# Linear attention and an MLP in one kernel: v of the first wave loaded and cast by the GpSimd queue

## The chip, the core and the metric

The kernel runs on one core of a Trainium2 chip. A core has a matrix engine (PE, with its weight loads shown apart as PEld), a vector engine (DVE), an activation engine (ACT), a general engine (GpSimd, POOL in the profile) and a sync engine (SP) that only issues transfers. The metric is the device time of one launch in microseconds, lower is better. Each engine works through its own list of instructions in order; an instruction may wait for another engine or for a transfer.

## What is computed

A causal linear attention with decay over 4 batches, 8 heads, 768 positions and 64 channels, and on its output an MLP of 512 to 2048 to 512:

```python
for b in range(nb):                      # blocks of 64 positions
    intra = np.einsum('bhic,bhjc->bhij', qb, kb) * Dmask[None]
    intra = np.einsum('bhij,bhjd->bhid', intra, vb)
    inter = np.einsum('bhid,bhde->bhie', qb * lam_pow[None], kv_state)
    out[:, :, sl] = intra + inter
    kv_state = lam_block * kv_state + np.einsum('bhsd,bhse->bhde', kb * rev_pow, vb)
x = out.transpose(0, 2, 1, 3).reshape(B * S, H * D)
h = x @ w_in
return (h * (1.0 / (1.0 + np.exp(-1.702 * h)))) @ w_out
```

Inputs and output are float32; the kernel multiplies in bf16.

## The kernel before

The positions are cut into six waves of 128 (NW = 6), and the 3072 rows of the MLP come 512 to a wave. Waves 0 and 1 are special (ND = 2): each holds the first 256 positions of two batches, called c = 0 and c = 1 in the code ("batch 0" and "batch 1" of the wave below). In them partition s holds the positions 2s and 2s + 1 next to each other, so that a transfer reads runs of 128 floats; a stands for the parity of the position. Waves 2 to 5 hold 128 positions of all four batches.

A pair (w, c) of the first two waves goes through these steps. `load_one` (L76) brings k, q and v as float32 on the SP queue; in wave 0 each comes in two halves of four heads (L79, L81), but v of batch 1 whole. `do_cast` (L193, L200) multiplies k and q by powers of the decay and writes bf16 (`ks`, `qs`). `cast_v` (L218) writes v in bf16 to `v_sb`, whose layout is partition, block, head, channel, with 2c + a as block: two copies, one for each parity, on the engines it is given (ACT at L216, GpSimd at L210). `turn_pe` (L227, L233) transposes `ks` and `qs` on PE and copies the result to `kT`, `qT`. `d_scores` (L246, L254) multiplies k by q and masks the product on DVE (`sm`, L258). `d_state` (L262, L269) makes the state from `ks` and v, for the first half of the positions and for all; `d_keep` (L275) copies it to `kv_sb` on ACT. `d_out` (L277) multiplies the masked scores by v (L284) and the state by q (L289), and `d_x` copies the sum to `xT`. Then the MLP can start for that batch's columns: `mlp1_half` (L370, L378) makes two of the 16 groups of hidden columns for half of the wave's rows, `mlp1` (L360, L366) one group for all, and `mlp2` (L384, L390) the output.

The order of work is written out by hand. Under `manual_schedule` the head (L432 to L485) lists wave 0 instruction by instruction; after it a list of side tasks with due places among the MLP's items sets the order (L506 to L537). `fill(n)` (L136, L140) issues n matmuls on zeros that nothing reads; they stand in the head where PE would else be idle.

Transfers are issued from two queues in the main: SP takes k, q, v, the DMA transposes of later waves and the stores; GpSimd takes the MLP's weights, which are cast from float32 to bf16 by the transfer (`load_w_in` L176, five pieces; `load_w_out` L181, four). Two gates hold a queue back: `gate_pool(x)` (L424) lets GpSimd read one element of x, so that what stands behind it on GpSimd starts when x is there; `gate_sync(x)` (L427) does it on SP with a tiny transfer. In the head GpSimd makes the masks and identity (L109 to L132), waits at the gate for the first half of v of batch 0 (L444), issues the first piece of w_in, casts k of batch 1 (L452), issues two pieces of w_in, casts one parity of v of batch 1, and then issues all other weights. SP loads all of wave 0 at once (L104) and waits before wave 1 until the second piece of w_out is there (L477).

Of the kernel before, what the change touches and what calls it, by code (L numbers as in the profile page):

```python
# [24 lines left out]
def kernel(  # L25
# [13 lines left out]
    nc = tc.nc  # L39
    f32 = mybir.dt.float32  # L40
    bf16 = mybir.dt.bfloat16
    B, H, S, D = q.shape
    P = 128
# [19 lines left out]
    const = ctx.enter_context(tc.tile_pool(name="const", bufs=1))  # L63
# [25 lines left out]
    def load(w, nms="kqv"):  # L89
        src = {"k": k, "q": q, "v": v}  # L90
        if w < ND:
            for c in range(HF):
                for nm in nms:
                    load_one(w, c, nm, src[nm])
        else:
            for nm in nms:
                for c in range(HF):
                    load_one(w, c, nm, src[nm])
# [2 lines left out]
    nc.scalar.dma_start(out=lam_r, in_=bass.AP(tensor=lam.tensor, offset=lam.offset, ap=[[0, 1], [1, H]]))  # L101
    ones = const.tile([1, P], f32)
    nc.vector.memset(ones, 1.0)
    load(0)  # L104

    nc.scalar.preload_act_table_set("natural_log_exp_and_others")

    def iota(x, pattern, base, cm):
        nc.gpsimd.iota(x, pattern=pattern, base=base, channel_multiplier=cm, allow_small_or_imprecise_dtypes=True)  # L109

    A, Z = slice(0, 64), slice(64, P)
    zero = const.tile([P, W], bf16)
# [3 lines left out]
    i_qd = const.tile([P, 2], f32)  # L116
    iota(i_qd[A], [[1, 2]], 1 - 2 * P, 2)
    iota(i_qd[Z], [[1, 2]], 1 - P, 2)
    ident = const.tile([P, P], bf16)
    make_identity(nc, ident)  # L120
    mask_d = const.tile([P, 1, 2, 2, D], bf16)
# [41 lines left out]
    mk_pow(blk_pow, 1.0 * P)  # L163
    warm = const.tile([P, 1], f32)

    v_sb = [const.tile([P, B, H, D], bf16, name=f"v_sb{i}") for i in range(2)]
    kv_sb = [const.tile([P, B, NP, P], bf16, name=f"kv{i}") for i in range(2)]

    CW = 4
# [45 lines left out]
    def act_copy(out, in_):  # L215
        nc.scalar.copy(out, in_)  # L216

    def cast_v(w, c, copies=(pool_copy, pool_copy)):  # L218
        f = loaded.pop((w, c, "v"))
        dst = v_sb[w % 2]  # L220
        if w < ND:
            for a in range(2):
                copies[a](dst[:, 2 * c + a], f.rearrange("p h (a d) -> p h a d", a=2)[:, :, a, :])
        else:
            copies[0](dst[:, 2 * c : 2 * c + 2].rearrange("p b h d -> p (b h d)"), f.rearrange("p h e -> p (h e)"))
# [34 lines left out]
            masked[w, c, pp, h] = sm  # L260

    def d_state(w, c, full, tag="a"):  # L262
        ks, vt, b = cast[w, c, "k"], v_sb[w % 2], 2 * w + c
        t, rows = acc("ps_kv", shape=[P, NP, D], tag=tag), slice(0, P) if full else A
        for r in range(NP):
            for a in range(2):
                for h, hs in enumerate((A, Z)):
                    n0 = r * P + h * D
                    nc.tensor.matmul(t[hs, r, :], ks[rows, a, n0 : n0 + D], vt[rows, 2 * c + a, 2 * r + h, :],  # L269
                                     start=(a == 0), stop=(a == 1))  # L270
        return t, b, 0 if full else 1

# [2 lines left out]
            nc.scalar.copy(kv_sb[i][hs, b, :, hs], t[hs, :, :])  # L275

    def d_out(w, c, tag="a"):  # L277
        vt, b = v_sb[w % 2], 2 * w + c
        oa, oz = acc("ps_o", tag=tag), acc("ps_o", tag=tag)
        for r in range(NP):  # L280
            for a in range(2):
                for t, bs in ((oa, A), (oz, Z)):
                    for h, hs in enumerate((A, Z)):
                        nc.tensor.matmul(t[hs, r, :], vt[bs, 2 * c + a, 2 * r + h, :],  # L284
                                         masked[w, c, r // 2, h][bs, r % 2, a, :], start=(r + a == 0),
                                         stop=(t is oa and a == 1), skip_group_check=True)
        for r in range(NP):
            for hs in (A, Z):
                nc.tensor.matmul(oz[hs, r, :], kv_sb[1][:, b, r, hs], q_of(w, c, slice(0, P), r, 1), start=False, stop=True,  # L289
                                 skip_group_check=True)  # L290
        if w not in xT:
            xT[w] = xp.tile([P, NP, W], bf16, tag="x", name="xT")
        return oa, oz
# [130 lines left out]
    def gate_pool(x):  # L424
        nc.gpsimd.tensor_copy(behind_q, x)
# [4 lines left out]
    with tc.manual_schedule():  # L430
        u32 = mybir.dt.uint32
        for x in kv_sb:  # L432
            nc.vector.memset(x.rearrange("p b r s -> p (b r s)").bitcast(u32), 0)
        nc.scalar.activation(warm, q_pow[:, 0, 0:1], GELU)
        fill(5)
        for g in range(2):
            do_cast(0, 0, "k", nc.vector, g)
            turn_pe(0, 0, "k", act_copy, g)
            fill(2)
        for g in range(2):  # L440
            do_cast(0, 0, "q", nc.vector, g)
            turn_pe(0, 0, "q", act_copy, g)
            fill(2 - 2 * g)
        gate_pool(loaded[0, 0, "v"][0:1, 0, 0:1])  # L444
        load_w_in(0)
        cast_v(0, 0, (act_copy, act_copy))
        d_scores(0, 0, 0)
        fill(1)
        d_scores(0, 0, 1)
        fill(3)  # L450
        for g in range(2):
            do_cast(0, 1, "k", nc.gpsimd, g)  # L452
        for j in (1, 2):
            load_w_in(j)
        one = d_state(0, 0, False, "mm")
        two = d_state(0, 0, True, "mm")
        fill(1)
        d_keep(*one)
        d_keep(*two)
        oa, oz = d_out(0, 0, "mm")  # L460
        d_x(0, 0, 0, oa, act_copy)
        d_x(0, 0, 1, oz, act_copy)
        do_cast(0, 1, "q", nc.vector, 0)
        do_cast(0, 1, "q", nc.vector, 1)
        turn_pe(0, 1, "k", dve_copy)
        turn_pe(0, 1, "q", act_copy, 0)
        fill(2, True)
        turn_pe(0, 1, "q", act_copy, 1)
        fill(2)
        cast_v(0, 1, (act_copy, pool_copy))  # L470
        for j in range(3, len(IN_CH)):
            load_w_in(j)
        for j in range(NCH):
            load_w_out(j)
        nc.gpsimd.affine_select(mask, mask, pattern=[[0, 1], [1, P]], channel_multiplier=-1, base=0,
                                compare_op=mybir.AluOpType.is_ge, fill=0.0)
        gate_sync(w_out_sb[1][0:1, 0, 0:2])  # L477
        load(1)
        d_scores(0, 1, 0)
        mlp1_half(0, 0, 0)  # L480
        d_scores(0, 1, 1)
        fill(1)
        one = d_state(0, 1, False)
        two = d_state(0, 1, True)
        d_keep(*one)  # L485

        def finish(w, c, two=None):
            oa, oz = d_out(w, c)
            d_x(w, c, 0, oa, act_copy)
            d_x(w, c, 1, oz, dve_copy)  # L490
            if two:
                d_keep(*two)

        def start(w, c):
            for pp in range(2):
                d_scores(w, c, pp)
            d_keep(*d_state(w, c, False))

        def end(w, c):
            finish(w, c, d_state(w, c, True))  # L500

        def stores():
            for f in late:
                f()

        side, main = [(0, (finish, 0, 1, two))], []  # L506
        for w in range(NW):
            n = len(main)
            main += mlp_items(w)
            e = len(main)  # L510
            x = w + 1
            if x < ND:
                for c in range(HF):
                    t, d = n + 24 + 5 * c, n + 19 + 7.5 * c
                    side += [(d, (do_cast, x, c, "k", nc.vector)), (d + 1 + 0.5 * c, (do_cast, x, c, "q", nc.vector)),
                             (d, (cast_v, x, c)),
                             (t, (turn_pe, x, c, "k", (act_copy, dve_copy)[c])),
                             (t + 1 + c, (turn_pe, x, c, "q", (act_copy, dve_copy)[c])),
                             (t + 3, (start, x, c)), (t + 6 - c, (end, x, c))]
            elif x < NW:  # L520
                for c in range(HF):
                    tk, tq = (n + 2.1 + 2 * c, n + 4 + c) if x == ND else (n + 4 + 2 * c, n + 5 + 2 * c)
                    side += [(tk, (do_cast, x, c, "k", nc.vector)), (tk, (turn_dma, x, c, "k")),
                             (tq, (do_cast, x, c, "q", nc.vector)), (tq, (turn_dma, x, c, "q")),
                             (n + 6 + 2 * c, (cast_v, x, c))]
                if x == ND:
                    side += [(n + 7, (stores,))]
                t = n + 16
                side += [(t, (n_two, x, 0)), (t + 4, (n_two, x, 1)), (t + 9, (n_rest, x))]
            if w + 2 < NW:  # L530
                side += [(n + (12 if w else 20), (load, w + 2))]
        side.sort(key=lambda x: x[0])
        for i, (f, *a) in enumerate(main):
            while side and side[0][0] <= i:
                _, (g, *b) = side.pop(0)
                g(*b)
            f(*a)  # L537
# [30 lines left out]
```

## Time and profile before

| what | us |
|---|---|
| median of 5 runs | 210.99 |
| the five runs | 210.83 to 212.99 |
| the profiled execution | 211.34 |
| its span, first to last instruction | 209.3 |
| ACT casts of v (L216), three | 0.62 each |
| GpSimd cast of v (L210), 128 x 512 | 0.61 |
| load of k or q of 256 KB on SP, issue to landing, median | 3.3, 5.5 |
| w_in pieces on GpSimd, issue to landing in the head | 5.0 to 9.5 |

The profile is one execution, 0.35 us above the median. A line of its timeline has the start and the duration in microseconds, the engine, the line of the kernel, the operation, what is written and read, how many instructions are merged, and in brackets how long the engine was idle before and what released it. The "chain that ended last" is followed back from the last instruction; it names PE for 90% of the span, the two full MLP lines alone for 70%. In the head it runs through the fillers, the transposes, the qT copy, the scores, the state and its copy, the output and the first MLP matmuls, and PE waits in the head for nothing longer than 0.5 us once it has begun.

### The profile page before, as it was taken

What the parts mean: (1) busy time and instruction counts of PE and PEld (TensorE: products, weight loads), DVE (VectorE), ACT (ScalarE), POOL (GpSimd) and SP (SyncE); (2) the same over time, 40 slices, a digit from 0 to 9 for tenths busy, and PEclk for the clock granted to TensorE, in tenths of its full rate; (3) what the DMA queues carried; (4) which work ended last, traced back from release to release, by engine and by line L of the source; (5) the groups of instructions that cost most, each with busy time, mean ns of one, the idle gap of its engine ahead of it and who ended that gap; (6) DMA issues with size and microseconds to landing.
All of it is one profiled execution on the core that took longest, in us unless ns stands there. A gap on an engine that the chain in (4) does not pass through costs nothing.

```text
span 209.3 us, 4272 instructions
## 1 busy us (share of the span) xinstructions
PE 201.7 (96%) x1810; PEld 107.7 (51%) x1835; DVE 94.6 (45%) x134; ACT 85.3 (41%) x156; POOL 24.2 (12%) x41
## 2 busy tenths in 40 slices
PE   7989999999999999999999999999999999999994
PEld 2567544557864464444464444464444464444453
DVE  5575000589931838851748720748720741100121
ACT  5886662223765030466030466030466021466000
POOL 4287000111030000510003000021000000000000
PEclk9999999999999999999999999999999999999999
DMA  5999999999998899999998499990480021100112
GB/s 144 303 246 199 202 207 262 290 263 213 189 203 169 186 231 215 229 187 172 223 217 196 138 180 214 228 247 2 135 168 0 24 81 50 50 0 3 50 50 100
DMA packets 87640, 33.82 MB, mean 162 GB/s; under 512 B 67398, under 2 KB 84678, under 8 KB 87622
## 3 DMA queue, kind: packets, MB, share of 16 engines
q1 hardware_dynamic: 82868, 29.37, 66.9%
q0 software_dynamic: 4752, 4.19, 12.6%
q8 instruction: 14, 0.23, 0.5%
q14 instruction: 4, 0.03, 0.0%
q10 hardware_dynamic: 2, 0.00, 0.0%
HBM read 27.26 MB, written 6.29 MB: 160 GB/s over the span
## 4 chain that ended last, share of the span: by engine, by line
PE 90%; DVE 5%; DMA 1%; issue 1%; ACT 1%; DVEq 0%
PE ps_out L390 37%; PE ps_h L366 33%; PE ps_h L378 5%; PE ps_fill L140 4%; PE ps_s L305 2%; PE ps_o L351 2%; PE ps_o L354 2%; PE ps_t L233 2%; DMA qT<-qs 1%; DVE o_sb L394 1%; DVE sm L258 1%; PE ps_o L284 1%; PE ps_s L254 1%; PE ps_kv L269 1%; PE ps_kv L329 1%
## 5 line engine op out<-in xcount | busy, mean ns | idle before, releaser
L390 PE MATMUL ps_out<-w_out,g_sb 128*128 128x512 bf16 (+2 forms) x400 | 83.8, 362 | 1.2 <-issue 0.8
L366 PE MATMUL ps_h<-xT,w_in 128*128 128x512 bf16 x330 | 73.2, 379 | 0.3
L368 ACT ACTIVATE g_sb<-ps_h 128x512 bf16<-128x512 f32 x84 | 50.2, 597 | 47.8 <-PE ps_h L366 47.8
L390 PEld LDWEIGHTS <-g_sb 128*128 128x128 bf16 x416 | 38.2, 98 | 41.0
L366 PEld LDWEIGHTS <-w_in 128*128 128x128 bf16 x336 | 32.9, 98 | 39.2
L394 DVE COPY o_sb<-ps_out 128x512 f32<-128x512 f32 (+2 forms) x26 | 16.9, 650 | 45.6 <-PE ps_out L390 45.5
L312 DVE SCALAR_TENSOR_TENSOR sm<-ps_s,inv_pow,mask 128x512 bf16<-128x512 f32 x32 | 21.8, 743 | 32.7 <-PE ps_s L305 24.7
L210 POOL CAST v_sb<-vf 128x1024 bf16<-128x1024 f32 (+1 forms) x13 | 12.4, 966 | 111.0 <-DMA vf<-in_v_dram 110.0
L358 ACT CAST xT<-ps_o 128x512 bf16<-128x512 f32 x16 | 8.2, 599 | 36.8 <-PE ps_o L354 36.8
L334 DVE SCALAR_TENSOR_TENSOR kv<-kv,blk_pow,ps_kv 64x256 bf16<-64x256 bf16 x24 | 11.5, 480 | 7.8 <-PE ps_kv L329 4.7
L200 DVE TENSOR_TENSOR ks<-kf,kd_pow 128x512 bf16<-128x512 f32 (+1 forms) x4 | 3.7, 955 | 18.9 <-DMA kf<-in_k_dram 17.6
L258 DVE TENSOR_TENSOR sm<-ps_s,mask_d 128x512 bf16<-128x512 f32 x16 | 10.0, 684 | 3.4 <-PE ps_s L254 3.2
L378 PE MATMUL ps_h<-xT,w_in 128*128 128x256 bf16 x96 | 11.3, 273 | 0.0
L205 DVE TENSOR_TENSOR ks<-kf,k_pow 128x1024 bf16<-128x1024 f32 x8 | 10.6, 1325 | 0.1
L205 DVE TENSOR_TENSOR qs<-qf,q_pow 128x1024 bf16<-128x1024 f32 x8 | 10.6, 1322 | 0.0
L140 PE MATMUL ps_fill<-zero 128*128 128x512 bf16 x22 | 8.8, 511 | 1.4 <-DVE zero L113 1.4
L378 PEld LDWEIGHTS <-w_in 128*128 128x128 bf16 x96 | 8.9, 98 | 1.7 <-DMA w_in<-in_moe_w_in_dram 0.2
L380 ACT ACTIVATE g_sb<-ps_h 128x512 bf16<-128x512 f32 x12 | 7.2, 597 | 4.7 <-PE ps_h L378 4.5
L351 PE MATMUL ps_o<-qT,kv 128*64 128x128 bf16 x128 | 7.7, 220 | 0.4
L351 PEld LDWEIGHTS <-kv 128*64 128x64 bf16 x128 | 7.0, 110 | 1.7 <-issue 1.7
L354 PE MATMUL ps_o<-sm,v_sb 128*64 128x128 bf16 x128 | 7.6, 219 | 0.0
L275 ACT CAST kv<-ps_kv 64x256 bf16<-64x256 f32 x16 | 5.9, 367 | 3.2 <-PE ps_kv L269 3.0
(59 smaller groups left out, 91.6 us busy)
## 6 DMA issues: line engine op xcount, KB each, us to landing
vf<-in_v_dram SPq DMA_DIRECT2D x11, 512.0 KB, 7.5
kf<-in_k_dram SPq DMA_DIRECT2D x10, 512.0 KB, 6.2
qf<-in_q_dram SPq DMA_DIRECT2D x10, 512.0 KB, 7.4
out_dram<-o_sb SPq DMA_DIRECT2D x15, 256.0 KB, 2.0
out_dram<-o_sb SPq DMA_DIRECT2D x17, 128.0 KB, 2.5
w_out<-in_moe_w_out_dram POOLq DMA_DIRECT2D x4, 512.0 KB, 14.0
w_in<-in_moe_w_in_dram POOLq DMA_DIRECT2D x3, 512.0 KB, 8.0
kf<-in_k_dram SPq DMA_DIRECT2D x4, 256.0 KB, 3.3
```

What stands on the lines that cost most here:

```text
L140: nc.tensor.matmul(fill_ps[0], zero[:, 0:P], zero, start=True, stop=True)
L205: eng.tensor_tensor(x.rearrange("p b (h d) -> p b h d", h=H), f.rearrange("p (b h) (a d) -> p b (h a) d", b=2, a=2), pw.unsqueeze(3).to_br ...
L210: nc.gpsimd.tensor_copy(out, in_)
L258: nc.vector.tensor_tensor(sm.rearrange("p i a s -> p i (a s)"), s2[h].rearrange("p (i a) s -> p i (a s)", i=2), mask_d.rearrange("p o a b ...
L312: nc.vector.scalar_tensor_tensor(sm, s, inv_pow[:, 2 * p + h : 2 * p + h + 1], mask.to_broadcast([P, B, P]), op0=MUL, op1=MUL)
L351: nc.tensor.matmul(ps_o[hs, b, :], kv[:, b, p, hs], qT[:, (b % 2) * NP + p, :], start=(b == 0), stop=False, skip_group_check=True)
L354: nc.tensor.matmul(ps_o[hs, b, :], vt[:, b, 2 * p + h, :], masked[w, p, h][:, b, :], start=False, stop=True, skip_group_check=True)
L366: nc.tensor.matmul(h, w_in_sb[j][:, kc, i * P : (i + 1) * P], xT[w][:, kc, :], start=(kc == 0), stop=(kc == KC - 1))
L368: nc.scalar.activation(g_of[w][:, fc, :], h, GELU)
L378: nc.tensor.matmul(h[:, u, :], w_in_sb[j][:, kc, i * P : (i + 1) * P], xT[w][:, kc, cols], start=(kc == 0), stop=(kc == KC - 1))
L390: nc.tensor.matmul(ps_out, g_of[w][:, fc, g * P : (g + 1) * P], w_out_sb[j][:, fc % CW, c0:c1], start=(fc == 0), stop=(fc == FFC - 1))
L394: nc.vector.tensor_copy(o, ps_out)
```

## The change

Three things change, all in wave 0. v of both batches is no longer loaded by SP and cast by ACT and GpSimd: a transfer on the GpSimd queue (`load_v`) casts it and writes it to `v_sb[0]`. It is written as it lies in memory, so that in wave 0 the parity stands inside the head, and `d_v` picks the matching slice for the matmuls. The first such transfer stands after GpSimd's iotas for q, the second behind a gate on the second half of k of batch 0; the gate before the first piece of w_in is on the second half of q of batch 0, where it was on v. SP loads k and q of batch 0, then k and q of batch 1, each in two halves. The list for batch 1 of wave 0 is also written in another order: both halves of q are transposed one after the other, two fillers come off there, the second scores stand ahead of the first `mlp1_half`, and the filler behind them comes off.

```diff
-    load(0)
+    load(0, "kq")
...
+    v_sb = [const.tile([P, B, H, D], bf16, name=f"v_sb{i}") for i in range(2)]
+
+    def load_v(c):
+        nc.gpsimd.dma_start(out=v_sb[0][:, 2 * c : 2 * c + 2].rearrange("p a h d -> p (a h d)").rearrange(
+            "p (h e) -> p h e", h=H), in_=v[c, :, 0 : 2 * P, :].rearrange("h (s a) d -> s h (a d)", a=2))
...
     iota(i_qd[Z], [[1, 2]], 1 - P, 2)
+    load_v(0)
...
+    def d_v(w, c, a, hd):
+        x = v_sb[w % 2][:, 2 * c : 2 * c + 2].rearrange("p a h d -> p (a h d)")
+        return x.rearrange("p (h a d) -> p a h d", h=H, a=2)[:, a, hd] if w == 0 else v_sb[w % 2][:, 2 * c + a, hd]
...
-                    nc.tensor.matmul(t[hs, r, :], ks[rows, a, n0 : n0 + D], vt[rows, 2 * c + a, 2 * r + h, :],
+                    nc.tensor.matmul(t[hs, r, :], ks[rows, a, n0 : n0 + D], d_v(w, c, a, 2 * r + h)[rows],
...
-                        nc.tensor.matmul(t[hs, r, :], vt[bs, 2 * c + a, 2 * r + h, :],
+                        nc.tensor.matmul(t[hs, r, :], d_v(w, c, a, 2 * r + h)[bs],
...
-        gate_pool(loaded[0, 0, "v"][0:1, 0, 0:1])
+        gate_pool(loaded[0, 0, "k"][0:1, H - 1, 0:1])
+        load_v(1)
+        gate_pool(loaded[0, 0, "q"][0:1, H - 1, 0:1])
         load_w_in(0)
-        cast_v(0, 0, (act_copy, act_copy))
...
         turn_pe(0, 1, "q", act_copy, 0)
+        turn_pe(0, 1, "q", act_copy, 1)
         fill(2, True)
-        turn_pe(0, 1, "q", act_copy, 1)
-        fill(2)
-        cast_v(0, 1, (act_copy, pool_copy))
...
         d_scores(0, 1, 0)
+        d_scores(0, 1, 1)
         mlp1_half(0, 0, 0)
-        d_scores(0, 1, 1)
-        fill(1)
```

## The prediction

> **What bounds the kernel now.** I read the page's busy shares first, then its 40 slices, then the timeline of the TensorE (PE) and of GpSimd (POOL) from 8 to 20 us, and last the DMA queues in narrow windows. Page, parts 1 and 2 (a digit is tenths of a 5.2 us slice):
>
> ```profile
> PE 201.7 (96%) x1810; PEld 107.7 (51%) x1835; DVE 94.6 (45%) x134; ACT 85.3 (41%) x156; POOL 24.2 (12%) x41
> PE   7989999999999999999999999999999999999994
> DMA  5999999999998899999998499990480021100112
> ```
>
> PE is busy 96% of 209.3 us, and all digits below 9 except the last lie in the first three slices. From about 19 us on, MLP matmuls run back to back to the end, so whatever moves the start of that run moves the end by as much. The change touches only what lies before it, and there the DMA row is at 9 as well. PE's timeline there (start, duration, engine, line, operation, count, and in brackets the idle time before):
>
> ```profile
> 10.22 0.82 PE L140 MATMUL ps_fill<-zero 128*128 128x512 bf16 x3
> 10.97 0.81 PE L269 MATMUL ps_kv<-v_sb,ks 64*64 64x64 bf16 x32
> 12.25 0.64 PE L284 MATMUL ps_o<-sm,v_sb 64*64 64x128 bf16 x32 [0.47 <-ACT kv L275]
> 14.50 0.59 PE L140 MATMUL ps_fill<-zero 128*128 128x512 bf16 x2
> 15.03 0.42 PE L254 MATMUL ps_s<-qT,kT 64*64 64x128 bf16 x16
> 15.47 1.05 PE L378 MATMUL ps_h<-xT,w_in 128*128 128x256 bf16 x8
> 16.80 0.39 PE L140 MATMUL ps_fill<-zero 128*128 128x512 bf16 x1
> 18.95 1.27 PE L378 MATMUL ps_h<-xT,w_in 128*128 128x256 bf16 x10
> ```
>
> See that no long hole is left: fillers (L140) stand directly before ps_kv, the first user of v. The run that must not stop begins at 18.95 (19.01 in the chain of waits). Now the loads. GpSimd's timeline, and ACT's v casts:
>
> ```profile
> 8.23 0.18 POOL L425 COPY behind_q<-vf 1x1 f32<-1x1 f32 x1 [4.85 <-DMA vf<-in_v_dram]
> 8.35 0.92 POOL L178 DMA_DIRECT2D w_in<-in_moe_w_in_dram  x1
> 10.13 2.04 POOL L200 TENSOR_TENSOR ks<-kf,kd_pow 128x512 bf16<-128x512 f32 x2 [0.86 <-DMA kf<-in_k_dram]
> 12.12 1.55 POOL L178 DMA_DIRECT2D w_in<-in_moe_w_in_dram  x2
> ...
> 9.70 1.14 ACT L216 CAST v_sb<-vf 128x512 bf16<-128x512 f32 x2
> ```
>
> And the queues' packets (count, MB, share), first 9.3 to 12 us, then 13 to 14, then 14 to 16:
>
> ```profile
> q1 hardware_dynamic: 1553, 0.77, 120.3%
> q0 software_dynamic: 3, 0.00, 0.4%
> ...
> q0 software_dynamic: 247, 0.13, 92.2%
> q1 hardware_dynamic: 217, 0.10, 45.5%
> ...
> q0 software_dynamic: 733, 0.38, 141.2%
> ```
>
> q1 is SP's queue, q0 GpSimd's. The first w_in had been issued at 9.27, yet to 12 us only 3 packets of it moved against 1553 of SP's; GpSimd's queue came in as SP's ran dry.
>
> **The change, part by part.**
>
> (1) SP's list falls from twelve units of 256 KB to eight (v's four go). 1553 packets in 2.7 us are 575 per us, so a unit of 512 packets takes 0.89 us. Today the eighth unit is batch 1's k, second half, in place when GpSimd's second cast of it began at 11.1. So SP's queue would end near 11.0 instead of 14.2 if nothing else shared the engines. Bytes read stay the same: the 1 MB of v now goes through GpSimd's queue.
>
> (2) Two v loads on GpSimd's queue, 1024 packets each of 512 B read and 256 B written; no row shows that form. Nearest rows: w_in's 1 KB reads, 733 packets in 2 us on 16 engines, 44 ns per packet and engine; 2 KB reads (20 to 30 us, 2041 packets), 78 ns; SP's own 512 B, 28 ns. These lie on one line in bytes read, so I take 28 ns: 64 packets per engine, 1.8 us a load. Lower end 19 ns (the write alone, half the bytes on that line), upper 59 (double and more, if the cast has a fixed price). Issue cost on GpSimd: 0.75 us for 512 packets, so 0.75 to 1.5 each; I take 1.2. The first is put after the iotas (1.31), and pushes identity, mask_d, i_k, i_q, mask to about 4.6: identity is first needed at 5.84, i_k by ACT at 5.02, mask_d at 9.73. Covered; without this cover up to 1.2 us. The second stands behind a gate on k's second half (landed by 5.4) and ahead of the w_in gate, now on q's second half (cast at 7.29) where it was on v's first (8.23). So w_in is issued about 0.8 earlier, but queues behind both v loads; GpSimd's k casts and later weight loads follow as before.
>
> (3) ACT loses three v casts (1.14 + 0.62), GpSimd one (0.61). Before ps_kv the ACT casts end at 10.84, the fillers at 11.04: the gain on the path is nothing, the fillers cover it. The later casts (14.42 to 15.81) end before 17.12, where their user starts: nothing again, except that GpSimd issues later weights 0.6 us earlier. Weights have slack: the fourth column group of w_in is needed at 21.6.
>
> (4) Three fillers less (two before L254 at 15.03, one at 16.80), 0.216 us each: 0.65 off the path. What is late next: the second scores need ACT's qT copy, done at 15.29, some 0.15 later than PE would be there. Net -0.5 if every load is where it is today. The second scores also stand ahead of the first half MLP now; its w_in (15.47 today) is then needed only at about 15.7.
>
> (5) v inside the head by parity: PE's reads stay 64 elements contiguous and the counts are equal. Zero.
>
> When does the first v land? Here **rule and row differ**. The row: w_in issued at 8.35, moving from 12, 3.7 us later, only as SP's queue emptied. The Trainium skill ("DMA: Bandwidth & Descriptors", Queues, rings and completion order; and Latency and other measured facts) says that each DMA engine goes round-robin between queues packet by packet, and gives about 1 us to the first byte for the GpSimd path; it also says that issuing from several engines adds no bandwidth. By the rule v alternates with k and q and delays both; by the row it waits for them. Taking the row: v flows freely from about 11.0, less some 0.4 us of it moved where SP leaves room (4.5 to 5.5 us: 424 packets against 623 per us just after), plus 1.8 and 0.3 for completion: 12.7, and 12.3 if the tails overlap as at 13 to 14 us. I take 12.3. Then ps_kv starts 1.3 after its 11.04. Batch 1's k and q have landed long before, so the rest follows at PE's pace: +1.3 - 0.65 + 0.25 (ACT's kv, xT and qT copies now run right behind one another) = **+0.9**. Second v 14.2, first w_in 15.7, needed at 17: no further wait.
>
> The profiled execution is 209.3 of span in 211.34; the five runs have the median 210.99, 0.35 lower. I add to the median: 211.9.
>
> The **clock** is the second place. The PE rows show the first fillers at 0.43 us and those from 8 us on at 0.21; the granted clock says 1.00 throughout. The skill ("TensorE: Matmul & The Clock Gate", The HAM clock gate) has the array fall back to half rate after an idle window of about 3.4 us. PE's new hole, 11.0 to 12.3, is far under that, so I charge nothing; by an idle window it would be up to 1.7 us more.
>
> **Rivals.**
>
> *B: the queues alternate.* v reaches the engines at 1.31 + 3.75 = 5.1. From there about 165 of SP's packets per engine are left, and alternate with 64 + 64 of v and 32 of w_in: 128 x 56 ns + 32 x 72 ns = 9.5, so batch 1's q, second half, lands at about 15.2 instead of 12.1. Then cast 0.65, transposes 0.3, fillers and copy 0.7, scores 0.4, half MLP 1.05, states 0.74, outputs 1.08: 20.3, **+1.3**, 212.3. For it: the rule, and 29 packets against 532 from 12 to 13. Against: 3 against 1553.
>
> *C: v slips in where SP leaves room.* If v comes by 10.9 and q stays under 13.5, only the fillers count: **-0.5**, 210.5. For it: DMA at half in the first slice, and the dip at 4.5.
>
> *S: slower, the price of a cast packet.* With 59 ns a v load is 3.8 us: v at 14.5, 18.3, first w_in 19.7, then 1.05 + 0.74 + 1.08: 22.6, **+3.6**, 214.6. It passes 1% from about 54 ns. Against: the three rows on one line.
>
> *It doesn't do what it says* is A itself: v "straight to its place" later than by way of ACT.
>
> **How the numbers follow.** A 0.42 (211.9), B 0.23 (212.3), C 0.20 (210.5), S 0.13 (214.6), 0.02 for something faster that I don't see. One per cent, 2.1 us, is about what a measurement of this kernel can tell from no change. Slower than 213.1: most of S (0.11) and 0.05 from A or B with a slow clock, 0.16. Faster than 208.9: 0.02. Within: 0.82. The range takes C less 0.3 at the bottom and B plus 1.0 (a price of 44 ns, or part of a cold window) at the top: 210.2 to 213.3.
>
> **What would show it.** Right if ps_kv's first matmul waits for v's DMA until about 12.3, SP's last head load is issued by about 6.5, and the first full MLP group starts near 19.9. B: DVE waits for q of batch 1 past 14. C: no wait before ps_kv. S: w_in lands after 17. Wrong altogether if the span grows after 25 us, in a stage that I hold untouched.

## The result, and the profile after

The changed kernel takes 212.65 us in the median of 44 runs (211.84 to 213.98), the kernel before on the same chips 211.58 (79 runs, 210.65 to 215.73). The ratio is 1.0049, with a 95% interval from 1.0035 to 1.0064: about 1.04 us are lost, less than one per cent. Ratios, here and below, leave out runs more than 1.5% above the fastest of their kernel. The forecast of +0.9 us was right in size (its 211.9 stood on a base of 210.99 from five runs, and the base is 211.58), and its mechanism was not: this is rival B. The profiled execution of the changed kernel took 212.98 us, with a span of 211.2 (before: 211.34 and 209.3). That pair differs by 1.64 because the one lies 0.33 above its median and the other 0.24 below its own.

The page of the changed kernel, parts 1 and 2:

```profile
PE 200.3 (95%) x1807; PEld 106.9 (51%) x1832; DVE 93.8 (44%) x134; ACT 83.5 (40%) x153; POOL 25.6 (12%) x43
PE   7588999999999999999999999999999999999993
DMA  5999999999999899999996399990480011100112
```

PE has 1.4 us less to do and the span is 1.9 us longer. In PE's row the second digit falls from 9 to 5 and the fourth from 9 to 8, and from the fifth on only the last differs: the loss lies in the first four slices, 21 us. The timeline of the changed kernel there, PE first, then DVE, then GpSimd:

```profile
8.89 0.40 PE L243 MATMUL ps_t<-ident,qs 128*128 128x128 bf16 x4 [1.39 <-DVE qs L206]
10.72 0.40 PE L243 MATMUL ps_t<-ident,qs 128*128 128x128 bf16 x4 [0.99 <-DVE qs L206]
12.14 0.82 PE L147 MATMUL ps_fill<-zero 128*128 128x512 bf16 x3
12.89 0.81 PE L279 MATMUL ps_kv<-v_sb,ks 64*64 64x64 bf16 x32
16.30 0.40 PE L243 MATMUL ps_t<-ident,qs 128*128 128x128 bf16 x4 [0.37 <-DVE qs L206]
17.72 1.05 PE L388 MATMUL ps_h<-xT,w_in 128*128 128x256 bf16 x8
20.75 2.79 PE L388 MATMUL ps_h<-xT,w_in 128*128 128x256 bf16 x24
...
8.14 0.69 DVE L206 TENSOR_TENSOR qs<-qf,qd_pow 128x512 bf16<-128x512 f32 x1 [2.08 <-DMA qf<-in_q_dram]
9.97 0.69 DVE L206 TENSOR_TENSOR qs<-qf,qd_pow 128x512 bf16<-128x512 f32 x1 [1.13 <-DMA qf<-in_q_dram]
15.55 0.69 DVE L206 TENSOR_TENSOR qs<-qf,qd_pow 128x512 bf16<-128x512 f32 x1 [0.41 <-DMA qf<-in_q_dram]
...
1.47 1.06 POOL L114 DMA_DIRECT2D v_sb<-in_v_dram  x1 [0.15 <-issue]
4.79 0.92 POOL L114 DMA_DIRECT2D v_sb<-in_v_dram  x1
10.08 0.62 POOL L435 COPY behind_q<-qf 1x1 f32<-1x1 f32 x1 [4.36 <-DMA qf<-in_q_dram]
10.65 0.75 POOL L184 DMA_DIRECT2D w_in<-in_moe_w_in_dram  x1
```

And the casts of q in the kernel before, from its DVE timeline:

```profile
6.35 0.69 DVE L200 TENSOR_TENSOR qs<-qf,qd_pow 128x512 bf16<-128x512 f32 x1 [0.29 <-DMA qf<-in_q_dram]
7.29 0.69 DVE L200 TENSOR_TENSOR qs<-qf,qd_pow 128x512 bf16<-128x512 f32 x1 [0.25 <-DMA qf<-in_q_dram]
12.13 1.28 DVE L200 TENSOR_TENSOR qs<-qf,qd_pow 128x512 bf16<-128x512 f32 x2
```

`ps_kv`, the first user of v, stands directly behind its fillers with no bracket: it waits for no v. What is late is q. DVE waits for all the halves of q shown; the two of batch 0 are cast at 8.14 and 9.97 (before 6.35 and 7.29), and the last one of batch 1 at 15.55 (before, both halves of batch 1 were cast in one stretch that ended at 13.41). The gate for w_in, which the change put on q, opens at 10.08. GpSimd's casts of batch 1's k stand behind it and move back too, to 11.42 and 12.67, but PE comes to them at 15.08 and does not wait. The MLP's run that must not stop starts at 20.75, 1.8 us after the 18.95 of before, and from there to the end of the span it is 190.4 us in both. The chain that ended last, followed back in the changed kernel (start, duration, what):

```profile
5.46 10.07 DMA qf<-in_q_dram
15.53 0.02 issue
15.55 0.70 DVE qs L206
...
17.53 2.48 DVE sm L268 x4
...
20.82 2.73 PE ps_h L388 x24
```

In the kernel before, the head of this chain was PE's own work. Now ten microseconds of it are one q load of 256 KB on SP's queue. The queues say why. Packets, MB and share in the window from 5.5 to 9 us, first before, then after, each its own fence:

```profile
q1 hardware_dynamic: 2182, 1.08, 114.3%
```

```profile
q1 hardware_dynamic: 1176, 0.58, 69.2%
q0 software_dynamic: 796, 0.20, 57.8%
```

SP's queue (q1) had the engines to itself and now moves little more than half as many packets; GpSimd's queue (q0) moves v beside it. Together they move 1972 packets in 3.5 us, so 28.4 ns a packet on each of 16 engines, as against 25.7 for SP alone. So about a tenth of the packet rate is lost; SP's own packets fall by 46%, and most of what k and q went without is what v took.

### The profile page after: what moved, and what is told of

Its sections match the earlier page's. It is cut to its first block, busy times and chain, and to the rows that moved or that the text cites. A ratio compares the mean times of both kernels' runs of the same rounds, so it can differ in the third digit from the quotient of the medians.

```text
span 211.2 us, 4262 instructions
## 1 busy us (share of the span) xinstructions
PE 200.3 (95%) x1807; PEld 106.9 (51%) x1832; DVE 93.8 (44%) x134; ACT 83.5 (40%) x153; POOL 25.6 (12%) x43
## 4 chain that ended last, share of the span: by engine, by line
PE 84%; DVE 6%; DMA 5%; SPq 2%; issue 1%; DVEq 0%
PE ps_out L400 37%; PE ps_h L376 34%; DMA qf<-in_q_dram 5%; PE ps_h L388 4%; DVE sm L268 2%; PE ps_s L315 2%; SPq L81 2%; PE ps_o L361 2%; PE ps_o L364 2%; DVE o_sb L404 1%; DVE qs L206 1%; PE ps_kv L339 1%; PE ps_t L243 1%; DVE ks L206 1%; PE ps_s L264 1%
## 5 line engine op out<-in xcount | busy, mean ns | idle before, releaser
L216 POOL CAST v_sb<-vf 128x1024 bf16<-128x1024 f32 (+1 forms) x12 | 11.4, 958 | 111.8 <-DMA vf<-in_v_dram 89.4
L211 DVE TENSOR_TENSOR ks<-kf,k_pow 128x1024 bf16<-128x1024 f32 x8 | 9.8, 1228 | 0.1
L147 PE MATMUL ps_fill<-zero 128*128 128x512 bf16 x19 | 7.2, 498 | 1.4 <-DVE zero L119 1.4
```

Source lines behind the costliest of these rows:

```text
L211: eng.tensor_tensor(x.rearrange("p b (h d) -> p b h d", h=H), f.rearrange("p (b h) (a d) -> p b (h a) d", b=2, a=2), pw.unsqueeze(3).to_br ...
L216: nc.gpsimd.tensor_copy(out, in_)
```

## The experiments

The two theories at this point: *the order* (the rewritten list for batch 1, or the fillers taken out), and *the sharing* (v on a second queue halves SP's pace). The first four kernels separate them, and within the second they ask whether GpSimd's queue takes turns or waits.

**The order alone**, in the kernel before:

```diff
         turn_pe(0, 1, "q", act_copy, 0)
-        fill(2, True)
         turn_pe(0, 1, "q", act_copy, 1)
-        fill(2)
+        fill(2, True)
...
         d_scores(0, 1, 0)
-        mlp1_half(0, 0, 0)
         d_scores(0, 1, 1)
-        fill(1)
+        mlp1_half(0, 0, 0)
```

> The kernel before with only batch 1's new order (q transposed in one go, three fillers less, both scores ahead of the first half MLP); v stays on the sync queue with its ACT and GpSimd casts. If the queues' sharing costs what the change loses, this order alone gains: the first full MLP group about 0.5 us earlier than 19.0, ratio to before 0.997 to 0.999. Rival, that the order itself loses (the first half MLP stands behind the second scores): 1.002 to 1.006.

Measured: ratio 0.9997 [0.9971, 1.0024], median 211.35 us. The order costs nothing that can be measured, and the gain that I expected, 0.997 to 0.999, is neither shown nor excluded. Its profiled execution, at 213.44 us near the top of its runs, waits for a weight instead (PE's timeline):

```profile
16.82 1.05 PE L378 MATMUL ps_h<-xT,w_in 128*128 128x256 bf16 x8 [1.17 <-DMA w_in<-in_moe_w_in_dram]
```

PE comes earlier to this load for want of fillers, but in this execution the load is also late: w_in was issued at 9.04, in the kernel before at 8.35. So this trace does not show what the order does by itself.

**v alone**: the changed kernel with the order and the fillers of before.

```diff
-        turn_pe(0, 1, "q", act_copy, 1)
         fill(2, True)
+        turn_pe(0, 1, "q", act_copy, 1)
+        fill(2)
...
-        d_scores(0, 1, 1)
         mlp1_half(0, 0, 0)
+        d_scores(0, 1, 1)
+        fill(1)
```

> The changed kernel with batch 1's old order and its three fillers back: v on the GpSimd queue alone. If the sharing of the DMA engines is the loss: q of batch 1 still lands near 15.5, and the MLP starts at 21.0 to 21.6, later than the changed kernel's 20.8; ratio 1.006 to 1.010. If the order is the loss: no slower than before, 0.998 to 1.002.

Measured: 1.0034 [1.0012, 1.0056]. The loss comes with this part. The interval overlaps that of the whole change, so the two cannot be told apart; that the loss would be larger with the old order, 1.006 to 1.010, was a miss. DVE's timeline shows q late here too, 9.06 and 14.96, where the full change had 9.97 and 15.55 and the kernel before 7.29 and, for the last half, about 12.8:

```profile
9.06 0.69 DVE L206 TENSOR_TENSOR qs<-qf,qd_pow 128x512 bf16<-128x512 f32 x1 [1.35 <-DMA qf<-in_q_dram]
14.96 0.69 DVE L206 TENSOR_TENSOR qs<-qf,qd_pow 128x512 bf16<-128x512 f32 x1 [1.08 <-DMA qf<-in_q_dram]
```

**One more load**: the kernel before, with a cast load of v of batch 0 on GpSimd's queue into a tile that nobody reads. It does not change what is computed, and it takes nothing off SP.

```diff
+    extra = const.tile([P, H, 2 * D], bf16)
+    nc.gpsimd.dma_start(out=extra, in_=v[0, :, 0 : 2 * P, :].rearrange("h (s a) d -> s h (a d)", a=2))
```

> The kernel before with one more load: v of batch 0 brought once more by the GpSimd queue, as the change does it, into a tile that nothing reads. If the queues alternate packet by packet: q of batch 0 lands 1 to 2 us later (first scores after 10), all later loads about 1.9 us later. If the sync queue goes first: k, q and v land where they are now, and only the first w_in comes 1.8 us later. Both make the span 1.5 to 2.2 us longer; the landing of q tells.

If SP went first, q of batch 0 could not notice this load. DVE's timeline, then the queues from 5.5 to 9 us:

```profile
7.79 0.69 DVE L202 TENSOR_TENSOR qs<-qf,qd_pow 128x512 bf16<-128x512 f32 x1 [1.74 <-DMA qf<-in_q_dram]
9.59 0.69 DVE L202 TENSOR_TENSOR qs<-qf,qd_pow 128x512 bf16<-128x512 f32 x1 [1.11 <-DMA qf<-in_q_dram]
```

```profile
q1 hardware_dynamic: 1211, 0.60, 70.4%
q0 software_dynamic: 784, 0.20, 56.0%
```

q is 1.4 and 2.3 us later than in the kernel before, and the split is that of the changed kernel to within 3%. Both queues move at once; neither waits for the other to run dry. This kernel shows it alone, with SP's list unchanged. That the turns go packet by packet is not seen: the trace does not say which engine a packet ran on. The time of this kernel, 216.08 us from a single run, is not used, because w_in came so late that PE stood still 1.95 us (PE's timeline), and the granted clock was at 0.50 from 20.0 to 23.4 us:

```profile
19.32 1.27 PE L380 MATMUL ps_h<-xT,w_in 128*128 128x256 bf16 x8 [1.95 <-DMA w_in<-in_moe_w_in_dram]
```

**v behind gates**: if the sharing is the loss, v should be let in when k and q of batch 0 are there.

```diff
-    load_v(0)
...
         gate_pool(loaded[0, 0, "k"][0:1, H - 1, 0:1])
-        load_v(1)
+        load_v(0)
         gate_pool(loaded[0, 0, "q"][0:1, H - 1, 0:1])
+        load_v(1)
         load_w_in(0)
```

> The changed kernel with each v load on the GpSimd queue issued one gate later: v of batch 0 behind k's second half, v of batch 1 behind q's. If v's packets alternate with those of k and q wherever both wait: q of batch 0 back near 7.3 (landed about 9.9 in the changed kernel), v of batch 0 about 12, q of batch 1 at 13.5 to 14.5, MLP start 19.5 to 20.2, ratio 1.000 to 1.004. If instead a fixed price of the GpSimd queue's cast packets is the loss, only the order of arrivals changes: last landing of q as late as 15.5 and ratio 1.005 or more.

Measured: 1.0077 [1.0052, 1.0103], a miss. q of batch 0 is back, as expected: its halves are cast from 6.65 to 8.2. But v, issued at 4.76, moved its first packet at about 8.0 and landed at 13.2. PE's timeline, and below it the windows of 2 us (stretch, sum, then busy time of PE, weight loads, DVE, ACT, POOL with their counts, granted clock, DMA share, GB/s):

```profile
13.18 1.21 PE L278 MATMUL ps_kv<-v_sb,ks 64*64 64x64 bf16 x32 [2.71 <-DMA v_sb<-in_v_dram]
```

```profile
10.00:12.00 2.00, 0.47 (x3) 0.10 (x1) 2.00 (x4) 0.00 (x0) 2.00 (x3) 1.00 1.51 218
12.00:14.00 2.00, 0.82 (x26) 0.75 (x27) 1.10 (x2) 0.15 (x1) 2.00 (x3) 0.64 1.55 183
14.00:16.00 2.00, 1.53 (x50) 1.33 (x46) 0.00 (x0) 1.33 (x5) 2.00 (x4) 0.50 1.41 193
16.00:18.00 2.00, 2.00 (x23) 1.83 (x23) 0.39 (x1) 1.16 (x2) 2.00 (x4) 0.50 1.16 181
18.00:20.00 2.00, 1.64 (x40) 1.06 (x39) 0.57 (x2) 1.07 (x2) 0.09 (x1) 0.66 1.22 199
```

The wait that my forecast saw for the change itself is here, 2.71 us long, and with it the granted clock falls from 1.00 to 0.50, by these rows for 6.8 us in all. `ps_kv` takes 1.21 us where it took 0.81. The MLP starts at 22.96. This execution took 215.27 us and has a mean granted clock of 0.984, like the two others of its 17 that took over 215 us. Twelve have 0.990 to 0.992, so they lost about half as much (an estimate from the means); two kept 0.999 and 1.00, and took 212.28 and 211.68 us, where the kernel before beside them has a median of 211.70. The forecast of 1.000 to 1.004 holds for these two alone: it left the clock out.

**The hole filled**: the same kernel with twelve more fillers before `ps_kv`.

```diff
-        fill(3)
+        fill(15)
```

> The run with the v loads issued one gate later, and twelve more fillers in front of the first state matmuls, where PE stood still 2.71 us for v and then ran at a granted clock of 0.5 to 0.66 until 20 us. If that hole is what took the clock: the clock stays at 1.00, the MLP starts near 20.5 instead of 22.96, ratio to before 1.002 to 1.005 (it was 1.0077). If the clock fell for another reason: ratio 1.007 or more, clock below 1 again.

Measured: 1.0046 [1.0016, 1.0077]. The profiled execution took 219.55 us and ran at a clock of 0.95 from about 7.4 us to the end, so only the order of its events is read: v is no earlier (`ps_kv` at 13.48), the clock does not fall to half there, and the MLP starts at 20.88. The intervals of the two kernels overlap, but their clocks do not: the other eleven runs of the filled kernel have a mean clock of 0.997 or more, which without the twelve fillers only two of 17 had. The fillers are the only difference between the kernels. They ran on different chips, but on the chip of the unfilled one none of the 20 runs of "v alone" is below 0.997. So it was the hole that took the clock. Even filled, this version only equals the change: v late costs about what q late costs.

**Is it the clock in the change too?** The changed kernel has holes of 1.39 and 0.99 us before the transposes of q. They are filled here:

```diff
-            fill(2)
+            fill(2 + 6 * g)
...
-            fill(2 - 2 * g)
+            fill(6 - 6 * g)
```

> The changed kernel with six more fillers before the first transposes of q and four more before the second, where PE stood still 1.39 and 0.99 us. Its profile shows a clock of 1.00, so with late loads as the only loss the ratio stays at 1.004 to 1.006. Rival, that part of its runs lose the clock in these holes: 1.001 to 1.003, with fewer runs above 213.

Measured: 1.0050 [1.0026, 1.0074], the change's own ratio. The rival is out: of the 44 runs of the change itself one has a mean clock of 0.992 and all others 0.997 or more. Filling these holes gives nothing back, because PE waits for q in any case.

**Is it the cast?** The same queues and gates, but v moves as float32 and is cast by ACT and GpSimd as before (new order).

```diff
-        nc.gpsimd.dma_start(out=v_sb[0][:, 2 * c : 2 * c + 2].rearrange("p a h d -> p (a h d)").rearrange(
-            "p (h e) -> p h e", h=H), in_=v[c, :, 0 : 2 * P, :].rearrange("h (s a) d -> s h (a d)", a=2))
+        x = ld.tile([P, H, 2 * D], f32, tag=f"v{c}", name="vf")
+        nc.gpsimd.dma_start(out=x, in_=v[c, :, 0 : 2 * P, :].rearrange("h (s a) d -> s h (a d)", a=2))
+        loaded[0, c, "v"] = x
...
+        cast_v(0, 0, (act_copy, act_copy))
...
+        cast_v(0, 1, (act_copy, pool_copy))
```

> The changed kernel's queues and gates with the cast taken out of the transfer: v comes as float32 on the GpSimd queue, and ACT and GpSimd cast it as in the kernel before. If the sharing of engines costs, not the cast: q of batch 0 lands at 9 to 10 as in the changed kernel, ratio 1.004 to 1.008. If the casting transfer's packets (40 ns each in the changed kernel, 27 to 34 on the sync queue) are the price: packets near 27 to 34 ns, q of batch 0 earlier by 0.5 or more, ratio 1.000 to 1.003.

Measured: 1.0101 [1.0063, 1.0140] from 4 runs, above both forecasts. The queues from 5.5 to 7 us, in the changed kernel and in this one:

```profile
q0 software_dynamic: 447, 0.11, 77.3%
q1 hardware_dynamic: 335, 0.17, 50.3%
```

```profile
q0 software_dynamic: 93, 0.34, 68.4%
q1 hardware_dynamic: 225, 0.11, 29.5%
```

Without the cast GpSimd's packets hold about 4 KB (0.34 MB in 93) and take some 180 ns each, as against 41 for the cast ones. In these 1.5 us SP moves 225 packets instead of 335. But from 7 to 9 us it is the other way, 1051 and 841, and from 5.5 to 9 us SP moves 1276 without the cast and 1176 with it. The MLP starts at 20.80 here and at 20.75 in the changed kernel. So the traces show the same loss with and without the cast: it is the sharing that costs. Why the ratio is higher is not shown; its interval touches that of the change, and one of the four runs has a mean clock of 0.989.

**Half of it**: v of batch 0 stays on SP, cast by ACT; only v of batch 1 goes on GpSimd's queue, behind the first w_in (new order).

```diff
-    load(0)
+    for c in range(HF):
+        for nm in ("kqv", "kq")[c]:
+            load_one(0, c, nm, {"k": k, "q": q, "v": v}[nm])
...
         load_w_in(0)
+        load_v(1)
...
-        cast_v(0, 1, (act_copy, pool_copy))
```

> Batch 1's new order, v of batch 0 on the sync queue with its ACT casts as before, only v of batch 1 on the GpSimd queue, issued behind the first piece of w_in. If what matters is that nothing on the GpSimd queue shares the engines with the loads that PE needs next: q of batch 0 as before, first w_in no later than 15.4, MLP start 18.3 to 18.7, ratio 0.996 to 0.999. If any v on the GpSimd queue costs: q of batch 1 lands past 13.5, ratio above 1.001.

Measured: 0.9993 [0.9977, 1.0009]. The MLP does start earlier, at 17.68, but the end does not move with it. PE's timeline and the chain that ended last:

```profile
17.68 2.79 PE L388 MATMUL ps_h<-xT,w_in 128*128 128x256 bf16 x24
21.34 10.53 PE L376 MATMUL ps_h<-xT,w_in 128*128 128x512 bf16 x47 [0.87 <-DMA w_in<-in_moe_w_in_dram]
```

```profile
15.53 16.80 DMA w_out<-in_moe_w_out_dram
...
32.34 0.77 SPq L438
...
33.60 6.66 DMA qf<-in_q_dram
40.28 1.24 DVE qs L202
```

Of the 1.27 us won at the start, 0.69 are there before the two kernels differ on PE, at the first scores (8.51 for 9.20), and PE's own speed is part of that. Two fillers took, here and in the kernel before:

```profile
5.95 0.59 PE L142 MATMUL ps_fill<-zero 128*128 128x512 bf16 x2
```

```profile
6.26 1.06 PE L140 MATMUL ps_fill<-zero 128*128 128x512 bf16 x2
```

PE starts slow in every profile here, and how soon it turns fast differs between executions; so a start in one profile can be early by luck. Of what was won, 0.87 go at once to a weight that has not landed. The rest is lost behind `gate_sync`: it passes at 32.34, in the kernel before at 30.30, and q of wave 1 is then what DVE and the chain wait for. So what is late next are the weights and, behind them, wave 1's q.

**The gate on the first piece of w_out**, with that version and in the kernel before alone:

```diff
-        gate_sync(w_out_sb[1][0:1, 0, 0:2])
+        gate_sync(w_out_sb[0][0:1, 0, 0:2])
```

> The run with only batch 1's v on the GpSimd queue, and the gate before wave 1's loads one piece of w_out earlier (first piece instead of second). There the MLP started at 17.68 instead of 18.95 but nothing of it reached the end; the chain of waits ran through w_out's landing at 32.3, the gate and wave 1's q. If that gate is where the gain went: wave 1's q is cast by 38, ratio to before 0.994 to 0.998. If the weights in front of it (the wait for w_in at 21.3) set the end: 0.998 to 1.001.

> The kernel before with that earlier gate alone. If in the kernel before PE sets the end between 31 and 52 us, the earlier loads are hidden: 0.999 to 1.001. If the wait for wave 1's loads costs it already: 0.995 to 0.998, and the run beside it owes its gain to the gate alone. Rival: wave 1's loads alternate with the last two pieces of w_out and delay them past 37: above 1.002.

Measured: 0.9997 [0.9962, 1.0031] and 1.0019 [0.9987, 1.0052]. Nothing is won: the gate passes at 28.14 and 29.08, but k and q of wave 1 then take 8.4 to 10.3 us to land in the median where they took 6.2 to 7.5 in the kernel before. No version tried beats the kernel before.

## Why the prediction was right in size and wrong in mechanism

*The bound and the place: right.* The MLP's run starts 1.8 us later and the span grows by 1.9; nothing after it moves (190.4 us in both).

*Step (1), SP's list ends near 11: wrong.* It held only "if nothing else shared the engines". The last q of batch 1 landed at 15.53, and B's sign, that DVE waits for it past 14, is there.

*Step (2), the price: right.* I took 28 ns for a cast packet and 1.2 us for the issue; the runs give 28.4 ns as the mean of both queues in the mixed window (an estimate of 32 for v's, if SP's keep their 25.7), and 1.06 and 0.92 us. S, which needed 54 ns, is out. That identity and masks, pushed back by the first issue, would be covered, held: they end at 4.6. "w_in is issued about 0.8 earlier" was wrong: its gate had been moved onto q, and q was late, so it was issued at 10.65 where it was 8.35. Its slack covered that; the half MLP at 17.72 waits for no weight.

*The choice between rule and row: this is the step that failed.* I read "3 packets against 1553" as SP going first. The Trainium skill ("DMA: Bandwidth & Descriptors", Queues, rings and completion order) says that an engine alternates between queues by packets; the row seemed to speak against it, and I followed the row. For the most part the row showed the time that GpSimd's queue needs before its first packet moves. After the change v was issued at 1.47 and began at 4.1, behind gates it was issued at 4.76 and began at 8.0, and w_in in the kernel before was issued at 8.35 and began at 11.8. That is 2.6 to 3.4 us whether SP's queue was at its beginning, in its middle or near its end. I had even used such a delay, 3.75 us, in B. Once begun, the queue moves beside SP's: 796 packets against 1176 in 3.5 us, and 784 against 1211 with the extra load. A row with few packets of a queue in it tells of a priority only when that queue is known to have begun.

*A, ps_kv waits 1.3 us for v: did not happen.* The first v landed 9.2 us after the start of its issue at 1.47, so at about 10.7, before even the 11.04 at which the fillers had ended in the kernel before; and q's lateness pushed `ps_kv` to 12.89. That +0.9 was forecast and +1.04 came out is a coincidence of two mechanisms.

*B, as it happened.* q's last cast ends 2.83 us later than before (16.24 for 13.41). The new order gives 1.03 back between there and the MLP (4.51 us for 5.54): 0.65 are the three fillers of step (4); the rest I put down to the work of batch 0, which is long done by then, without a test. 2.83 - 1.03 = 1.80, the delay of the MLP in this pair of profiles. B had 20.3 for its start and it was 20.75. B was not exact in its own sums: its terms add up to about 15.0 for the landing of q, where it has 15.2, and from 15.2 on to 20.1, where it has 20.3. By its terms it was short by 0.5 us for q and by 0.3 for the rest.

*C, v in SP's gaps: out.* In the first slice there was room, but the start-up took it: from 2 to 4.5 us GpSimd's queue moved 31 packets, SP's 1201.

*Step (3), casts removed are worth nothing, and step (5), the layout: held.* No wait in the head names ACT's casts, and `ps_kv` keeps its 0.81 us. *Step (4), net -0.5:* not measurable alone (0.9997).

*The clock: nothing charged, and rightly for this kernel.* The stop of 1.39 us in the changed kernel left the granted clock at 1.00, and 43 of its 44 runs have a mean of 0.997 or more, so nothing speaks for a charge on the 1.3 us that I expected. But the margin was smaller than I wrote. The skill ("TensorE: Matmul & The Clock Gate", The HAM clock gate) puts the idle window at about 3.4 us; in the gated kernel a stop of 2.71 us came with a clock of 0.50, and with the extra load one of 1.95 us did. Here the measurement decides.

*Open.* Runs of the kernel before at full clock spread from 210.7 to 213.5 us, and loads of the head land 0.5 to 0.8 us apart between executions of the same loads; what decides this was not found. A few runs of it lose some clock as well: in the lists beside the later kernels twelve of 132 have a mean clock of 0.991 or 0.992, and they took 213.5 to 214.2 us. It was not tried how long GpSimd's queue takes to begin when nothing else moves. Nor is its share even: in the kernel before it had begun at 11.8 and still moved only 29 packets beside SP's 532 from 12 to 13 us, and in the changed kernel 106 beside 572 from 9 to 10. Why is not known; of the row that misled me, this part stays unexplained.

## What to carry to other kernels

In this kernel a load moved to a second queue did not come free beside the first queue's loads, it came in between them (SP's packets fell from 2182 to 1176 in the same 3.5 us), and what was in order of need no longer was. Where the engines are full, as here, that is a reason to keep the loads that PE needs next in one queue in the order in which they are needed, and to ask of every load that comes earlier which one now comes later. A head start is worth something only if the next load in line, here the weights and the gate behind them, is early too.

## What the runs showed of the hardware that was not expected

- GpSimd's queue took 2.6 us (issue at 1.47), 3.3 us (at 4.76) and 3.4 us (at 8.35) from the start of the issue to the first packet, where the Trainium skill ("DMA: Bandwidth & Descriptors", Latency and other measured facts) gives about 1 us to the first byte; the two loads of v (256 KB written each) landed 9.2 and 10.2 us after the start of their issue, beside SP's loads.
- Both queues moved at once, and SP's own packets fell for it: with v on GpSimd's queue, or one more load there, they were 1176 and 1211 in 3.5 us, where SP alone moved 2182. With packets of 4 KB instead of short ones on GpSimd's queue they were 1276.
- A PE stop of 2.71 us took the granted clock to 0.50 for 6.8 us, and one of 1.95 us for 3.4 us; stops of 1.39 and 0.99 us left it at 1.00. The same stop does not cost the same in every run: of 17 runs of the gated kernel three have a mean clock of 0.984, twelve 0.990 to 0.992 and two 0.999 or more.
